# Linear attention and two MLPs on one core: rank of the weight sums and place of the key products

## The chip, the cores and the metric

The kernel runs on one core of a Trainium2 chip. The metric is the time of one execution on the device in microseconds (us), here as the median of several runs. The profile is one further execution, recorded instruction by instruction.

## What is computed

```python
kv  = einsum('bhsd,bhse->bhde', k, v)           # 8 batches, 8 heads, 576 rows, 64 columns
out = einsum('bhsd,bhde->bhse', q, kv)
x   = out / sqrt(mean(out**2, -1) + 1e-6) * g_norm
x   = x.transpose(0, 2, 1, 3).reshape(4608, 512)
h   = x @ w_in                                  # first MLP, 512 -> 2048 -> 512
g   = where(h >= 1, h, where(h <= -1, 0, (h + 1)**2 / 4))
x   = g @ w_out
h   = x @ w_in2                                 # second MLP, same sizes
out = maximum(h, 0)**2 @ w_out2
```

The weights come in as float64 and are narrowed on the chip; the rest is float32.

## The kernel before

**Blocks and pairs.** The 4608 rows are nine blocks of 512. Blocks 0 to 4 of the first MLP are computed plainly: for each of 16 slices of the hidden width, `h_stage` (line 686) makes 12 matmuls into a PSUM bank, then ScalarE and VectorE form the gate u (lines 704 to 706), `g_stage` (712) splits it into a high and a low part (gs), and `out_stage` (729) makes 12 more matmuls into four accumulators, two slices behind. Two rounds of hooks stand in one slice: a half slice is called a slot, so a block has 32 slots. The rest (blocks 5 to 8 of the first MLP, all of the second) is computed in pairs of blocks, with seven block products instead of eight (`in_phase`, 904, and `out_phase`, 969). For these pairs sums of quarters of the weights are needed.

**The weight sums.** They are made during blocks 1 to 4, in 16 units (`units`, line 1127; the loop that hooks them stands at 1134 to 1154). A unit loads two raw slices of the second MLP's weights (`prep_load`, 313), narrows them (`prep_narrow`, 345, through `narrow_w`, 267: one ScalarE and two VectorE instructions each, lines 272 to 275), forms four sums (`prep_sums`, 357: four VectorE instructions, lines 362 to 366), splits four tiles (`prep_split`, 369, through `split_halves`, 185: one ScalarE and one VectorE instruction each, the latter at line 189), and then does the same for the first MLP's weights, which lie in SBUF already: `prep_join` (332, line 342) adds their two parts again, `prep_sums`, and two splits. For the last slices of `w_out` the parts come back from DRAM, as tiles wf and wt. Each split tile is stored to DRAM (wsd) from ScalarE's queue two slots later (`owe` and `pay`, 173 to 182). The split tiles go round a ring of SBUF slots (`prep_ring`), which the tiles e of the first pair take over (`e_pairs`, line 776).

**The attention.** A block's attention is computed while the block before it runs, and that of blocks 5 to 7 inside the first two pairs ("hosted": two groups of six pairs of heads). `attention` (652) gives every job a slot: pair of heads j has its base s, 7 slots behind the one before it (6 in the hosted groups). At s - 7 the loads of k and v, at s the key product `kv_stage` (474; from block 2 on one call serves two pairs of heads, j and j + 1, and stands at j's slot) and the transpose of q, at s + 3 and s + 4 the two halves of the output (`o_stage`, 570: product po, squares, scaling), at s + 6 the sums of squares `r_stage` (596): product pr for two halves, logarithm (609), exponential (611), square, a Newton step on VectorE (526) that reads pr once more, and the normalisation. So the sums of squares of pair j - 1 stand at s - 1 of pair j (at s in the hosted groups, in front of j's key product). The product pkv is evicted in four pieces, each a ScalarE copy and a VectorE subtraction into kvbd (lines 497 to 499); po reads kvbd.

**Banks.** From block 1 on, pkv, po and pr all take their PSUM bank from one pool of two (`bank`, 397, tag `at`).

**What sets the order.** Each instruction has a rank, which counts up as the program is traced. When the program is built, the instructions of each engine are put in order by a planner that plays the program through: of the instructions that it holds to be ready it takes the one with the lowest rank. The order is fixed from then on; on the chip each engine and each DMA queue goes through its list and waits at its head.

Of the kernel before, what the change touches and what calls it, by code (L numbers as in the profile page):

```python
# [77 lines left out]
def linear_attention_rms_two_mlps(  # L78
# [19 lines left out]
    NF = DFF // P  # L98
# [5 lines left out]
    LAG = 2  # L104
    AHEAD = 3
    WARM = 11
    PACE = 0.75
    WAVE = 6
    WHOLE = ((1, 0), (1, 1))
    WARMS = ((0, 5), (6, 5), (8, 3), (12, 4), (14, 3), (20, 3), (26, 3))  # L110
# [22 lines left out]
    PLAIN = 5  # L133
# [518 lines left out]
    def attention(base, every, order):  # L652

        slots = []
        for j, (b, hp) in enumerate(order):
            s = base + int(every * j)
            turn.setdefault((b, hp), len(turn))
            if b == 1:
                slots += [(max(0, s - 7), load_kv, b, hp), (s, kv_stage, (b, hp))]
            elif j % 2 == 0:  # L660
                two = order[j : j + 2]
                turn.setdefault(two[-1], len(turn))
                slots += [(max(0, s - 7), load_kv, *i) for i in two]
                slots.append((s, kv_stage, *two))
            slots += [
                (max(0, s - (7 if b < PLAIN or j < 2 else 5)), load_q, b, hp),
                (s, t_stage, b, hp),
                (s + 3, o_stage, b, hp, 0),
                (s + 4, o_stage, b, hp, 1),
            ]  # L670
            if j == 0 and b < PLAIN:
                slots.append((s + 6, begin, b))
            slots.append((s + 6, r_stage, b, hp))
        if b < PLAIN:
            slots.append((2 * NF * b, store_xrem, b))
        return slots
# [398 lines left out]
    def outputs(n, hn, hm):  # L1075
# [21 lines left out]
                stores.append((rows[a], src))  # L1097
        return stores

    blocks = [(1, b) for b in range(PLAIN)]  # L1100
    hooks = {}

    def hook(s, f, *a):
        hooks.setdefault((s // 2, s % 2), []).append((f, a))

    jobs = [(8, store_xrem, 0)]
    for b in range(1, PLAIN):
        jobs += attention(2 * NF * (b - 1), 7, [(b, hp) for hp in range(NP)])
# [25 lines left out]
    for which, i, s0, j in [  # L1134
        (which, i, 2 * NF * (n + 1) + s, 4 if s in (0, 6, 12) else 6)
        for n in range(PLAIN - 1)
        for which, i, s in units[n]
    ]:
        for d, L, f, a in (
            (-6, 2, prep_load, ()),  # L1140
            (0, 2, prep_narrow, (0,)),
            (1, 2, prep_narrow, (1,)),
            (2, 2, prep_sums, ()),
            (2, 2, prep_split, (0,)),
            (3, 2, prep_split, (1,)),
            (3, 2, prep_split, (2,)),
            (4, 2, prep_split, (3,)),
            (2, 1, prep_load, ()),
            (j, 1, prep_join, ()),
            (j + 1, 1, prep_sums, ()),  # L1150
            (j + 1, 1, prep_split, (2,)),
            (j + 2, 1, prep_split, (3,)),
        ):
            hook(min(s0 + d, 2 * NF * PLAIN - 1), f, L, which, i, *a)

    first_x = x2_jobs(0, Ring(*[(st, "st")] * 7))
    when = [2, 3, 3, 4, 5, 6, 7, 8, 7, 9, 9, 10, 11, 12, 13, 14]
# [5 lines left out]
    for n in HOSTED:  # L1163
        for s, *job in sorted(attention(1, 6, HOSTED[n]), key=lambda j: j[0]):
            if s:
                in_pair.setdefault((n, s), []).append(job)
            elif n:
                in_pair.setdefault((n - 1, 14 * NQ - 4), []).append(job)
            else:
                hook(last + 25, *job)  # L1170
# [17 lines left out]
    for j in range(2):  # L1188
        s = slice(j * D, (j + 1) * D)
# [140 lines left out]
```

## Time and profile before

| | before |
|---|---|
| median of 3 runs | 1578.89 us (1577.68 to 1579.36) |
| profiled execution | 1579.17 us |
| its span, first to last instruction | 1577.4 us |
| TensorE busy | 98% |
| VectorE busy | 76% |
| ScalarE busy | 59% |
| mean granted clock of TensorE | 0.998 |

PE is TensorE's matmul, PEld its weight load, DVE VectorE, ACT ScalarE, SP the queue that issues most loads; a q behind an engine's name is its sequencer. L242 and the like are lines of the kernel (L242 and L880 are helpers that issue the matmuls of the blocks and of the pairs, L189, L221, L228 and L809 helpers for splits, copies and squares). An arrow to the left leads from what is written to what is read. Behind a wait stands what ended it.

### The profile page before, as it was taken

How to read it: one execution, taken by the hardware profiler on the slowest of the kernel's cores; microseconds unless marked ns; L12 is line 12 of the kernel's file. 1: busy time of each engine (PE TensorE's matmuls, PEld its weight loads, DVE VectorE, ACT ScalarE, POOL GpSimd, SP SyncE). 2: the span in 40 equal slices, each digit the busy share in tenths (PEclk: the TensorE clock that was granted, in tenths of full speed). 3: DMA queues.
4: the chain of work that ended last, by engine and by line, in shares of the span. 5: the costliest groups of instructions: out<-in, count | busy, mean ns of one | idle time of the engine just before them, and what ended most of it. 6: DMA issues, size and time to landing. Idle time of an engine off the chain costs nothing.

```text
span 1577.4 us, 22371 instructions
## 1 busy us (share of the span) xinstructions
PE 1542.1 (98%) x7631; PEld 1265.3 (80%) x7633; DVE 1196.6 (76%) x2112; ACT 929.3 (59%) x1751; POOL 13.0 (1%) x30
## 2 busy tenths in 40 slices
PE   9999899999999999998999999999999999999999
PEld 5787778878877788786778888888888888888899
DVE  6975878887989678965599788868884597559676
ACT  5976666766756567735576466546653464446354
POOL 0000000000000000000000000000000000000000
PEclk9999999999999999999999999999999999999999
DMA  9676899796899967778667877766777676977797
GB/s 284 201 246 200 263 319 317 247 286 207 271 346 348 323 202 223 243 211 239 197 211 233 224 244 236 227 218 195 245 225 212 196 244 196 244 239 226 218 390 247
DMA packets 330914, 388.17 MB, mean 246 GB/s; under 512 B 197808, under 2 KB 223408, under 8 KB 330800
## 3 DMA queue, kind: packets, MB, share of 16 engines
q1 hardware_dynamic: 299904, 330.63, 69.2%
q10 hardware_dynamic: 30896, 56.11, 9.5%
q8 instruction: 61, 1.00, 0.3%
q14 instruction: 53, 0.43, 0.1%
HBM read 300.42 MB, written 86.25 MB: 245 GB/s over the span
## 4 chain that ended last, share of the span: by engine, by line
PE 81%; DVE 8%; ACT 5%; DMA 4%; issue 1%; SPq 0%; ACTq 0%; DVEq 0%
PE ph L880 32%; PE po L880 28%; PE acc L242 9%; PE ph L242 8%; DMA ws<-wsd 1%; PE pkv L486 1%; PE po L242 1%; DMA wsd<-s 1%; DVE s L189 1%; PE pr L608 1%; DVE u L706 1%; DVE t L809 1%; DMA v<-in_v_dram 1%; DVE x L809 1%; DVE t L526 1%
## 5 line engine op out<-in xcount | busy, mean ns | idle before, releaser
L880 PE MATMUL ph<-x,ws 128*128 128x512 f32 (+1 forms) x2352 | 507.3, 376 | 0.5 <-DVE u L706 0.5
L880 PEld LDWEIGHTS ph<-x,ws 128*128 128x128 f32 x2352 | 419.6, 189 | 80.0 <-DVE u L706 0.9
L880 PE MATMUL po<-t,ws 128*128 128x512 f32 x2016 | 463.6, 390 | 1.6 <-DVE t L809 1.2
L880 PEld LDWEIGHTS po<-t,ws 128*128 128x128 f32 x2016 | 376.4, 188 | 84.7 <-DVE t L809 6.7
L809 DVE TENSOR_TENSOR t<-g,t 128x512 fp32r<-128x512 f32 (+1 forms) x336 | 216.0, 649 | 82.7 <-ACT t L221 75.9
L221 ACT CAST t<-g 128x512 fp32r<-128x512 f32 (+1 forms) x336 | 195.2, 590 | 115.9 <-PE po L880 62.2
L242 PE MATMUL ph<-x,w 128*128 128x512 f32 x960 | 240.2, 394 | 6.0 <-DVE u L706 4.5
L242 PEld LDWEIGHTS ph<-x,w 128*128 128x128 f32 x960 | 177.0, 188 | 49.3 <-DVE u L706 9.3
L242 PE MATMUL acc<-gs,w 128*128 128x512 f32 x528 | 133.3, 394 | 2.5 <-DVE u L706 1.5
L957 ACT ACTIVATE g<-h 128x512 f32<-128x512 f32 (+1 forms) x120 | 70.6, 589 | 99.0 <-DVE h L946 98.8
L242 PEld LDWEIGHTS acc<-gs,w 128*128 128x128 f32 x528 | 97.4, 188 | 24.5 <-DVE u L706 2.0
L946 DVE CUSTOM_DVE_ANT_0 h<-ph,e 128x512 f32<-128x512 f32 (+1 forms) x120 | 76.1, 637 | 53.5 <-PE ph L880 49.5
L936 DVE TENSOR_TENSOR e<-ph,e 128x512 f32<-128x512 f32 (+1 forms) x112 | 72.3, 650 | 57.1 <-PE ph L880 48.4
L242 PE MATMUL acc<-gs,wt 128*128 128x512 f32 x432 | 105.2, 390 | 2.8 <-DVE gs L234 1.7
L242 PEld LDWEIGHTS acc<-gs,wt 128*128 128x128 f32 x432 | 80.4, 188 | 19.9 <-DVE gs L234 2.1
L221 ACT CAST x<-xr 128x512 fp32r<-128x512 f32 (+1 forms) x98 | 57.4, 590 | 46.7 <-DVE xr L860 23.1
L221 ACT CAST gs<-u 128x512 fp32r<-128x512 f32 x80 | 49.8, 622 | 51.4 <-DVE u L706 42.3
L706 DVE SCALAR_TENSOR_TENSOR u<-u,ph 128x512 f32<-128x512 f32 x80 | 54.6, 682 | 22.7 <-ACT u L228 22.5
L704 ACT ACTIVATE u<-ph,halfb 128x512 f32<-128x512 f32 x80 | 55.3, 691 | 27.0 <-PE ph L242 17.4
L234 DVE TENSOR_TENSOR gs<-u,gs 128x512 fp32r<-128x512 f32 x80 | 55.0, 688 | 16.4 <-ACT gs L221 15.9
L933 ACT COPY e<-ph 128x512 f32<-128x512 f32 (+1 forms) x56 | 30.6, 553 | 58.6 <-PE ph L880 51.7
L809 DVE TENSOR_TENSOR x<-xr,x 128x512 fp32r<-128x512 f32 (+1 forms) x98 | 63.1, 648 | 2.5 <-ACT x L221 2.5
(135 smaller groups left out, 1620.7 us busy)
## 6 DMA issues: line engine op xcount, KB each, us to landing
ws<-wsd SPq DMA_DIRECT2D x392, 512.0 KB, 4.4
wsd<-s ACTq DMA_DIRECT2D x96, 512.0 KB, 5.6
wt<-wsd SPq DMA_DIRECT2D x36, 512.0 KB, 5.4
raw<-in_moe_w_in_dram SPq DMA_DIRECT2D x32, 512.0 KB, 6.9
raw<-in_moe_w_out_dram SPq DMA_DIRECT2D x32, 512.0 KB, 6.3
xr<-x1d SPq DMA_DIRECT2D x36, 256.0 KB, 5.3
out_dram<-ov SPq DMA_DIRECT2D x142, 64.0 KB, 3.7
wsd<-w SPq DMA_DIRECT2D x17, 512.0 KB, 4.0
```

What stands on the lines that cost most here:

```text
L189: lo.tensor_tensor(t[:, :, 1, :], src, t[:, :, 0, :].bitcast(F32), ALU.subtract)
L221: return e.copy(dst, src)
L234: lo = engine(op + "_lo", phase).tensor_tensor(t[:, 1, :], src, t[:, 0, :].bitcast(F32), ALU.subtract)
L242: nc.tensor.matmul(dst, wt(a), xt(c), start=first and n == 0, stop=last and n == 2)
L704: nc.scalar.activation(u, ps, AF.Relu, bias=halfb, scale=0.5)
L706: nc.vector.scalar_tensor_tensor(u, u, 1.0, ps, op0=ALU.min, op1=ALU.max)
L809: engine2(op + "_lo").tensor_tensor(t[:, 1, :], src, t[:, 0, :].bitcast(F32), ALU.subtract)
L880: nc.tensor.matmul(ps, wt(a), xt(c), start=first and n == 0 and i == 0, stop=last and n == len(lhs) - 1 and i == 2, skip_group_check=True,)
L933: nc.scalar.copy(e[i, 1], bank)
L936: nc.vector.tensor_tensor(e[i, p], bank, e[i, 1], ALU.add)
L946: nc.vector._custom_dve(TENSOR_ADD_SAT, out=h, in0=bank, in1=add, s0=float("inf"), s1=0.0)
L957: nc.scalar.activation(g, h, AF.Square)
```

## The change

Three edits. The 16 units' instructions, apart from the loads, are traced by way of `behind`, which gives them a rank 60 higher than the place at which they are traced. A key product that serves two pairs of heads, unless it is its group's first, is put one slot earlier in the hosted groups and two slots earlier in blocks 2 to 4, so that it is traced ahead of the sums of squares of the pair of heads before it. A constant that nothing reads (`PACE`) is replaced by `BEHIND`.

```diff
-    PACE = 0.75
+    BEHIND = 60
...
-                slots.append((s, kv_stage, *two))
+                slots.append((s - (1 if j else 0) - (b < PLAIN and j > 0), kv_stage, *two))
...
+    def behind(f, *a):
+        with tc.high_priority(offset=-BEHIND):
+            f(*a)
+
...
-            hook(min(s0 + d, 2 * NF * PLAIN - 1), f, L, which, i, *a)
+            if f is not prep_load:
+                f, a = behind, (f, L, which, i, *a)
+                hook(min(s0 + d, 2 * NF * PLAIN - 1), f, *a)
+            else:
+                hook(min(s0 + d, 2 * NF * PLAIN - 1), f, L, which, i, *a)
```

## Rows read from the trace of the kernel before

**Rows 1.** The page, busy time, share of the span and instructions

```profile
PE 1542.1 (98%) x7631; PEld 1265.3 (80%) x7633; DVE 1196.6 (76%) x2112; ACT 929.3 (59%) x1751; POOL 13.0 (1%) x30
```

**Rows 2.** Stretches (us): length, busy time of each engine, clock, DMA share, GB/s

```profile
core 0: us, PE busy (x) PEld busy (x) DVE busy (x) ACT busy (x) POOL busy (x), PEclk, DMA share, GB/s
...
125.70:235.00 109.30, 100.87 (x534) 79.53 (x532) 76.53 (x145) 68.91 (x136) 4.17 (x4) 1.00 0.86 269
235.00:335.00 100.00, 99.59 (x527) 82.11 (x527) 82.69 (x158) 69.72 (x139) 1.93 (x5) 1.00 0.90 281
...
431.30:523.30 92.00, 90.74 (x425) 72.72 (x424) 80.16 (x153) 58.77 (x106) 0.00 (x0) 1.00 1.01 347
...
710.00:830.00 120.00, 108.39 (x543) 88.53 (x542) 83.92 (x138) 70.76 (x144) 0.00 (x0) 0.97 0.76 218
```

**Rows 3.** TensorE's waits in block 1, 125.7 to 235: total, times, longest

```profile
PE ph L242 <- DVE u L706: 2.9, 4, 1.4
PE pr L608 <- ACT wk L213: 1.7, 2, 1.0
...
PE pr L608 <- DVE s2lo L594: 1.1, 1, 1.1
...
PE pkv L486 <- DVE t L526: 0.4, 1, 0.4
```

**Rows 4.** TensorE's waits in block 4 and behind it, 431.3 to 531

```profile
PE acc L242 <- DVE gs L234: 1.7, 1, 1.7
PE ph L242 <- DVE u L706: 1.2, 3, 0.7
```

**Rows 5.** TensorE's waits in the hosted stretch, 700 to 830

```profile
PE pkv L486 <- DVE t L526: 5.7, 2, 3.1
...
PE po L242 <- DVE kvbd L499: 1.4, 1, 1.4
PE po L242 <- ACT kvbd L221: 1.4, 1, 1.4
```

**Rows 6.** A stretch of the pairs, 900 to 1000, as rows 2

```profile
900.00:1000.00 100.00, 99.87 (x439) 81.78 (x438) 87.15 (x140) 64.27 (x107) 0.00 (x0) 1.00 0.78 240
```

**Rows 7.** TensorE in order of time, 738 to 757: start, length, in brackets idle before

```profile
744.75 0.56 PE L486 MATMUL pkv<-kv 128*64 128x64 f32 x10 [3.11 <-DVE t L526]
...
752.34 1.01 PE L242 MATMUL po<-qT,kvbd 128*128 128x288 f32 x3 [1.40 <-ACT kvbd L221]
```

**Rows 8.** The same, 786 to 797

```profile
785.82 2.90 PE L880 MATMUL ph<-x,ws 128*128 128x512 f32 x12
...
791.59 0.69 PE L486 MATMUL pkv<-kv 128*64 128x64 f32 x16 [2.61 <-DVE t L526]
...
792.69 0.29 PE L486 MATMUL pkv<-rest 128*64 128x64 f32 x4
```

**Rows 9.** Two stretches behind TensorE's waits, as rows 2

```profile
745.60:749.00 3.40, 3.40 (x10) 2.63 (x9) 2.25 (x4) 0.37 (x1) 0.00 (x0) 0.50 1.01 407
...
755.80:759.30 3.50, 3.50 (x10) 2.73 (x9) 0.76 (x1) 0.99 (x3) 0.00 (x0) 0.51 0.00 0
```

**Rows 10.** VectorE in order of time, 792 to 799.5

```profile
798.74 0.23 DVE L499 TENSOR_TENSOR kvbd<-pkv,kvbd 64x64 fp32r<-64x64 f32 x1
```

**Rows 11.** TensorE in order of time, 183 to 186

```profile
183.81 0.69 PE L486 MATMUL pkv<-v,k 128*64 128x64 f32 x16
```

**Rows 12.** SP's queue in order of time, 171 to 178.5

```profile
175.69 0.60 SPq L433 DMA_DIRECT2D rest<-in_v_dram  x1
```

**Rows 13.** The tile rest, 160 to 190

```profile
DMA to landing us min/median/max: 2.7/3.0/3.2
```

**Rows 14.** Groups of VectorE's instructions, 125.7 to 530: busy, mean ns | idle before

```profile
L189 DVE TENSOR_TENSOR s<-s,s 128x512 fp32r<-128x512 f32 x62 | 42.0, 684 | 13.7 <-ACT s L221 13.6
```

**Rows 15.** VectorE in order of time, 518 to 540

```profile
525.46 0.69 DVE L342 TENSOR_TENSOR j<-wt 128x512 f32<-128x512 f32 x1 [4.29 <-DMA wt<-wsd]
...
537.71 0.69 DVE L936 TENSOR_TENSOR e<-ph,e 128x512 f32<-128x512 f32 x1 [3.84 <-DMA wsd<-s]
```

## The prediction

> **What bounds the kernel now.** I read the shares of the engines first. TensorE is busy 1542.1 of 1577.4 us [rows 1], so all that a change of order can win is about 35 us, of which the first load and the last eviction keep some 5. The stage table says where TensorE loses time: 8.4 us in block 1 (109.30 long, 100.87 busy), 0.4 in block 2, 1.3 in block 4, 11.6 in the stretch 710 to 830 that carries the second half of the hosted attention; VectorE is at 70 to 87% in these stages, so it has slack on average and is late only in places [rows 2]. The waits of TensorE name the places. Block 1 waits for u and for the operands of the sums of squares [rows 3]; the end of block 4 waits once for gs and three times for u [rows 4]; the hosted stretch waits 5.7 us in two places for the key product's bank, and 2.8 for the split of its result [rows 5]. These waits, not an engine's total, set the end: TensorE's stream is fixed work with holes.
>
> A rule bears on how much room there is. In 900 to 1000 us, where TensorE is busy 99.87 of 100, its weight loads are busy 81.78 [rows 6]; 80% over the whole span [rows 1] is thus already the full pace. The Trainium skill (Perfetto Trace Analysis, Identifying the Most-Contended Engine) says that matmul busy time is no good measure of the distance to the roofline and that the share of LDWEIGHTS is; by it a fifth of the span, some 312 us, would be open, by the row only the 35.
>
> **The key product.** One product serves two pairs of heads. In each of the two hosted groups of six pairs, the second and the third product are moved one slot forward (4 in all); of blocks 2 to 4 each has its second product moved two slots (3, which run in blocks 1 to 3). Each brings 40 small matmuls, 4 ScalarE and 4 VectorE pieces of its eviction; its loads stay where they are. Nothing is added.
>
> Today the product is traced behind the sums of squares of the pair before. It needs one of the two attention banks, and these are held until VectorE's Newton step has read the sums of squares (L526), at the end of a chain of logarithm, exponential and square. So TensorE stands 3.11 us at 741.6 and 2.61 us at 789.0 [rows 7, 8]. In front of the sums it takes the bank of the output's first half, which ScalarE freed earlier: both waits go, -5.7 us.
>
> The first of them costs more than itself. Behind it the clock of TensorE is granted at 0.50 for 3.4 us, though it is busy throughout, and again at 0.51 for 3.5 us behind the two waits of 1.4 us [rows 9]; behind the 2.61 us wait it isn't. At 0.50 (1.2 instead of 2.4 GHz) 3.4 us hold 1.7 us of work, so each such stretch costs 1.7. The first goes with its wait: -1.7. The second, and the 2.8 us of waits on the split before it, come from a product that was late and evicted late; one slot (12 matmuls, 2.7 us, rows 8) earlier it should be out, unless ScalarE takes the pieces as late as now. Between 0 and -4.5 I take half: -2.3.
>
> What is late next is the second half of the sums of squares. Its bank can only be the key product's, since the first half's is held until both halves are through the chain. Today four pieces are out 7.4 us after the product starts (791.59 to 798.97) [rows 8, 10], in the middle of other work. The builder may put 12 or more other matmuls between, so the price is from 0 to 3.3 us each (7.4 less the product's own 1.4 and a slot of 2.7). I take 0.5, because TensorE's order is chosen at build time with these waits in view: 4 x 0.5 = +2.0.
>
> In blocks 2 to 4 the gain is the one wait there, 0.4 [rows 3]. Against it stand the loads: the product of block 2 runs at 183.81, but the last of its loads is issued at 175.69, and these land 3.2 us later at the slowest, 178.9 [rows 11 to 13]. Two slots, some 6 us, earlier it asks for them at 177.8: a wait of 1.1, with bounds of 0 and 4.6 (in front of the sums of squares, traced in the slot between, it could start as early as 174.3). In the other two blocks the loads land long before. Net +0.7.
>
> **The sums.** 16 units, each 8 ScalarE and 20 VectorE instructions, get a rank 60 traced instructions later, about two slots; one split piece takes 0.68 us [rows 14]. Their loads keep their rank, and so do the stores that ScalarE's queue issues, which now can wait there for a later split. A rank decides only where the builder finds several instructions ready; there u, gs and the attention now go first. Engine time doesn't change, VectorE's slack takes the delay, so I cost the delay itself at nothing in blocks 1 to 3; without that cover each late store would hold up a ring slot and the next unit. The gain is taken from the waits on u and on the sums of squares in block 1 and on u in block 4, 2.9 + 1.7 + 1.1 + 1.2 = 6.9 us [rows 3, 4]. A wait goes only where a sum stood in front at that moment; half: -3.4, between 0 and -6.9.
>
> At the end of block 4 I give nothing for the 1.7 us wait for gs. VectorE sits 4.29 us on a tail weight that the join of the last unit reads, with gs queued behind; yet 12 us later it sits 3.84 us until that unit's store has freed the slot that e of the first pair writes [rows 15]. TensorE gains 1.7 at the first place and arrives earlier at the second, which still hangs on the same load. If the last splits slip behind two more operations, 2 x 0.68, TensorE pays that: +1.4, between 0 and about 3.
>
> **The sum**: -5.7 - 1.7 - 2.3 + 2.0 + 0.7 - 3.4 + 1.4 = -9.0. The profiled execution took 1579.2 us (span 1577.4), 0.3 above the median of 1578.9, so the forecast is **1570.0 us**, -0.6%. About 0.2% (3.2 us) is what a measurement of this kernel can tell from no change.
>
> **Rivals.**
> (a) The ranks do nothing: sums stand where they stand because their inputs arrive when they do (the 4.29 us wait is one for a load, rows 15), not because of a tie. Then the last two terms fall away: -5.7 - 1.7 - 2.3 + 2.0 + 0.7 = -7.0, 1572. For it: blocks 2 to 4 have few waits with the same sums in them. Against: the wait on u in block 1, beside an idle that no load explains. Still faster.
> (b) The wait changes place: the second half of the sums waits 2 us at each of the four hosted products (8 us instead of the 2.0 that I charged) and the 2.3 doesn't come: 1570.0 + 6.0 + 2.3 = 1578.3. For it: two banks, and an eviction of 7.4 us. Against: TensorE's order is free to put other matmuls in.
> (c) Slower, by the same bank where the eviction stays as slow as the row: each of the four second halves waits the full 3.3 us, 13.2, and two of these waits lower the clock, 3.4. Against the forecast that is 13.2 - 2.0 + 3.4 = +14.6: 1584.6. It decides from where a wait passes about 2.7 us without the clock: 4 x 2.7 is the hosted gain of 9.7 and 1.3 from the sums. That is a product whose last piece comes over 6.8 us behind its start. For it: the 7.4 measured. Against: that eviction stood behind a late product, with nobody pressing it. The Trainium skill (Perfetto Trace Analysis, Matmuls) wants independent groups to rotate through banks so that the eviction of one overlaps the matmuls of the next; with two banks the moved product breaks that rotation, which speaks for this rival. No row of before shows a sum of squares behind a key product.
>
> **Chances.** The forecast's case 0.54 (1563 to 1575), (a) 0.14 (1570 to 1575), (b) 0.16 (1575.7 to 1582), (c) 0.16 (above 1582). Faster by over 0.2% is the first two, 0.68; within 0.2% 0.16; slower 0.16. Its best end is all of the hosted waits and clock (11.9) and most of the others: 1561. The range of 1561 to 1581 holds the first two cases and nearly all of (b), and leaves out (c); the forecast's own range is 1563 to 1575.
>
> **What would show it.** Right: no wait of a key product for L526 in the hosted stretch, the clock there at 1.00 instead of 0.97, and TensorE's idle time between 710 and 830 down from 11.6 to some 3; in block 1 waits on u under 1.5. Wrong, step by step: a wait of pr for kvbd (the bank's price is larger than 0.5); a wait of the key product for a load near 178 us (two slots too early); VectorE's order in block 1 with the sums still in front (the rank does nothing); a longer idle than 3.84 in front of the first pair's e with TensorE waiting behind (the late sums set the first pair's start). If idle of TensorE turns up in stages that now have none, the new order itself, which none of these terms holds, has made it.

## The result, and the profile after

The changed kernel is slower: median 1588.03 us (1586.32 to 1590.83) against 1578.29 us for the kernel before (1576.46 to 1579.36); ratio 1.0066, 95% interval 1.0051 to 1.008. By the ratio that is +10.4 us where -9.0 was forecast, and outside the range. The profiled execution took 1586.32 us, its span 1584.5, against 1577.4; mean granted clock 0.992 against 0.998.

The page's first part says that no engine got more to do; it answers to [rows 1].

```profile
PE 1542.3 (97%) x7633; PEld 1270.4 (80%) x7633; DVE 1198.8 (76%) x2112; ACT 932.3 (59%) x1751; POOL 10.4 (1%) x30
```

TensorE has the same busy time and 7 us more idle time. Where, the stretches from stage to stage show: block 1, block 4, the first pair with the first hosted group, and the 120 us behind it. Their columns are those of [rows 2].

```profile
core 0: us, PE busy (x) PEld busy (x) DVE busy (x) ACT busy (x) POOL busy (x), PEclk, DMA share, GB/s
125.92:233.15 107.23, 99.34 (x504) 79.84 (x502) 75.34 (x142) 68.45 (x133) 1.69 (x4) 0.98 0.84 269
...
430.35:526.54 96.19, 91.79 (x425) 74.37 (x424) 82.21 (x155) 58.40 (x103) 0.00 (x0) 0.98 0.96 333
526.54:711.01 184.47, 175.98 (x849) 144.35 (x848) 144.22 (x243) 107.77 (x212) 0.00 (x0) 0.97 0.76 233
711.00:831.00 120.00, 109.93 (x582) 89.72 (x581) 78.88 (x133) 68.41 (x141) 0.00 (x0) 0.97 0.74 209
```

The same stages in the kernel before, cut at the same matmuls of the blocks and pairs:

```profile
125.69:234.93 109.24, 100.81 (x534) 79.47 (x532) 76.47 (x145) 68.85 (x136) 4.17 (x4) 1.00 0.86 268
...
431.25:523.36 92.11, 90.85 (x425) 72.79 (x424) 80.20 (x153) 58.82 (x106) 0.00 (x0) 1.00 1.01 348
523.36:700.49 177.13, 174.13 (x849) 142.62 (x848) 141.77 (x237) 105.67 (x207) 0.00 (x0) 1.00 0.78 238
```

Block 1 gains 2.0 us, block 4 loses 4.1, the first pair loses 7.3, blocks 2 and 3 lose 0.4 each, and from the start of the second hosted group to the end 3.4 are gained (1577.4 - 700.49 against 1584.5 - 711.01). With 0.2 at the start that is the 7.1 of the span. Blocks 1 and 2 belong together: 30 small matmuls of a key product stand ahead of the cut between them in the kernel before and behind it in the changed kernel (534 and 504 instructions in block 1). And of the 3.4 only 1.5 are gained in the hosted group: counted by the matmuls of the pairs, the changed kernel is 10.5 us behind at 700, 9.1 at 849 and 7.1 at 1191 us of the kernel before, and between the last two no attention is computed. So the loss stands where the forecast had a +1.4, and the hosted gain, forecast at 7.7, is 1.5 in these two traces.

**The first pair.** TensorE's waits between 420 and 560 have one of 7.8 us that the kernel before does not have:

```profile
PE ph L880 <- DVE e L936: 7.8, 1, 7.8
PE ph L242 <- DVE u L706: 4.1, 3, 2.1
```

VectorE between 536 and 553, in order of time (idle before in brackets), stands in front of e for a store, as in [rows 15], but twice as long:

```profile
536.59 1.89 DVE L189 TENSOR_TENSOR s<-s,s 128x512 fp32r<-128x512 f32 x3 [0.71 <-ACT s L221]
546.39 0.69 DVE L936 TENSOR_TENSOR e<-ph,e 128x512 f32<-128x512 f32 x1 [7.91 <-DMA wsd<-s]
```

ScalarE's queue over the same time issues the stores of these splits:

```profile
535.92 1.67 ACT L221 CAST s<-s 128x512 fp32r<-128x512 f32 x3
537.31 2.69 ACTq L181 DMA_DIRECT2D wsd<-s  x3
```

The last unit's two splits end at 538.5, their stores are the last two of the three (issued at 539.0 and 539.5), and only when the first of these has landed is the ring slot free that e wants: e stands 7.4 us behind its issue. In the kernel before that store is issued at 532.04 and e stands at 537.71 [rows 15], 5.7 us behind it. The wait costs more than itself. Stretches as in [rows 9], the first behind a 2.05 us wait for u in block 4, the second behind this one, are at half the clock:

```profile
467.00:470.40 3.40, 3.40 (x10) 2.65 (x9) 3.40 (x7) 2.06 (x5) 0.00 (x0) 0.51 1.04 407
...
542.00:552.20 10.20, 5.07 (x12) 4.01 (x13) 3.53 (x8) 3.84 (x9) 0.00 (x0) 0.50 0.64 222
```

5.07 busy us at half the clock hold 2.5 us of work. 7.8 + 2.5 less the 1.7 that the kernel before waits for gs [rows 4] is 8.6, somewhat over the 7.3 that the stage lost (5.5 more idle and 1.9 more busy, by the rows above).

**The hosted stretch.** The two waits of the key product [rows 7, 8] are gone, and two others have come, seen in TensorE's order of time:

```profile
751.00 0.69 PE L486 MATMUL pkv<-kv 128*64 128x64 f32 x16
...
752.31 0.40 PE L608 MATMUL pr<-s,ones 128*128 128x288 f32 x1
752.55 0.29 PE L608 MATMUL pr<-s2lo,ones 128*128 128x288 f32 x1
752.68 2.91 PE L880 MATMUL ph<-x,ws 128*128 128x512 f32 x12
755.42 0.35 PE L608 MATMUL pr<-s,ones 128*128 128x288 f32 x1
...
759.79 0.67 PE L242 MATMUL po<-qT,kvbd 128*128 128x288 f32 x2 [3.89 <-ACT qT L221]
...
800.00 0.40 PE L608 MATMUL pr<-s,ones 128*128 128x288 f32 x1 [3.45 <-DVE kvbd L499]
```

At 800.00 the second half of the sums of squares waits for the key product's bank, as feared. At 752.68 it does not wait: the builder put 12 matmuls in between. But then the second half reads its squares (tile s2, tag wk2) 3 us later, and the transposed q of the next pair of heads goes into that same buffer:

```profile
755.35 1.29 DVE L946 CUSTOM_DVE_ANT_0 h<-ph,e 128x512 f32<-128x512 f32 x2
756.55 0.77 DVE L565 STREAM_TRANSPOSE qf<-q 128x576 f32<-128x576 f32 x1
```

In the kernel before that transpose runs at 741.76, 3.0 us ahead of the key product at 744.75; here 5.6 us behind it, and the output's product waits 3.89 us for it. At the second place VectorE is seen waiting, in front of the transpose, for the matmuls that read s2:

```profile
800.44 0.78 DVE L565 STREAM_TRANSPOSE qf<-q 128x576 f32<-128x576 f32 x1 [0.49 <-PE pr L608]
```

The 3.89 us are not the buffer's alone: the transpose ends at 757.3, and ScalarE casts its result only at 759.03, behind an exponential, a gate step and a square. In block 1 a wait of 4.25 us for the transposed q stands at 193.12.

**ScalarE in blocks 1 to 4.** A gate is two instructions on ScalarE, lines 704 and 228 (u), and ScalarE also issues the stores. Its waits in front of the second, 125 to 530, before:

```profile
ACT u L228 <- DMA v<-in_v_dram: 3.3, 1, 3.3
...
ACT u L228 <- ACT u L704: 0.7, 2, 0.4
```

and after:

```profile
ACT u L228 <- DVE s L189: 7.2, 7, 2.3
...
ACT u L228 <- DVE j L342: 5.2, 2, 3.1
ACT u L228 <- DMA wsd<-s: 4.7, 1, 4.7
...
ACT u L228 <- DVE s L366: 2.5, 1, 2.5
...
ACT u L228 <- DVE d L274: 1.6, 1, 1.6
```

4.0 us have become 23.4 (the rows left out are of 1.1, 0.9 and 0.2). The square needs none of the five shown: what stands between it and line 704 in ScalarE's list is a store, which waits, mostly for its split (in the row of 4.7, and in the 3.3 of before, for an earlier transfer to land). The stores kept their rank while the splits got a later one. In the list as built, 8 of the 64 gates of blocks 1 to 4 have such a store inside before, 27 after.

### The profile page after: what moved, and what is told of

Same layout as the page of the kernel before. It is cut to its first block, busy times and chain, and to the rows that moved or that the text cites. A ratio compares the mean times of both kernels' runs of the same rounds, so it can differ in the third digit from the quotient of the medians.

```text
span 1584.5 us, 22442 instructions
## 1 busy us (share of the span) xinstructions
PE 1542.3 (97%) x7633; PEld 1270.4 (80%) x7633; DVE 1198.8 (76%) x2112; ACT 932.3 (59%) x1751; POOL 10.4 (1%) x30
## 4 chain that ended last, share of the span: by engine, by line
PE 83%; DVE 6%; DMA 5%; ACT 4%; issue 1%; ACTq 0%; SPq 0%; DVEq 0%
PE ph L880 31%; PE po L880 28%; PE acc L242 10%; PE ph L242 9%; DMA wsd<-s 2%; DMA ws<-wsd 2%; PE po L242 1%; PE pkv L486 1%; PE pr L608 1%; DVE t L809 1%; PE pwarm L1191 1%; DVE x L809 1%; DMA rest<-in_k_dram 1%; DVE s L189 0%; ACT raw L272 0%
```

## The experiments

Each expectation was written before its run. The ratios are to runs of the kernel before on the same chip. Taken alone, the parts give:

| what differs from the kernel before | median us | ratio, 95% interval | ratio less 1, in us |
|---|---|---|---|
| the change | 1588.03 | 1.0066, 1.0051 to 1.008 | +10.4 |
| key products alone (e1) | 1579.49 | 1.0005, 0.9996 to 1.0015 | +0.8 |
| ranks alone (e2) | 1586.93 | 1.0048, 1.0034 to 1.0062 | +7.6 |
| ranks of blocks 1 to 3 alone (e14) | 1583.26 | 1.0021, 1.001 to 1.0032 | +3.3 |
| ranks of block 4 alone (e13) | 1584.03 | 1.0029, 1.002 to 1.0039 | +4.6 |
| rank of the last unit alone (e8) | 1578.77 | 1.0001, 0.9992 to 1.001 | +0.2 |

The second, fourth and fifth row make 8.7 together, inside the interval of the change (8.0 to 12.6).

### Key products alone, ranks alone

e1 is the kernel before with the changed line in `attention` alone; e2 with `behind` alone.

> Only the key products are moved; the sums keep the rank of before. Theory (late sums cost the time, the key products bring some 3 us in the hosted stretch): 1576 us, between 1573 and 1579, no wait of over 4 us of TensorE on e at the start of the first pair, and the waits of po for qT (4.2 in block 1, 3.9 in the hosted stretch) still there. Rival (the key products cost the time, since they push the sums of squares and with them the next transpose back): 1586 us or more, as the changed kernel.

Measured 1579.49 us, ratio 1.0005: nothing gained, between theory and rival. The hosted waits are those of the changed kernel (3.89 and 3.46), and nothing waits long for e. The moved products take two waits away and put two as long in their place. The wait for q's transpose in block 1, which the theory expected as well, is not there: it comes in runs that have both parts (the change, e3 with 4.25, e4 and e5), and in neither part alone.

> Only the sums get the later rank; the key products stand where they stood. Theory: the last unit's store comes some 7 us later than before, TensorE waits about 8 us on e at the start of the first pair and loses 5 more to the clock behind it: 1591 us, between 1586 and 1595. Rival (the key products cost it): 1576 to 1580 us.

Measured 1586.93 us, ratio 1.0048. TensorE waits 7.58 us for e at 540.29 and 4.34 for u at 463.57, and in the hosted stretch as before (3.11, 2.60, 1.40, 1.43). The loss is the ranks'. A first theory, on record together with these two, was that it is nearly all the ring's, some 13 us of wait and clock.

### The ring and the last unit, with the rest of the change

```diff
-    hook(last + 1, prep_ring.add, *((xp, f"x{KD + i}") for i in range(KD)))
+    def turn_ring():
+        prep_ring.slots[:] = [(wp, "w1_15")] + [(xp, f"x{KD + i}") for i in range(KD)]
+        prep_ring.slots += [(wp, f"w1_{i}") for i in (12, 13, 14)]
+
+    hook(last + 1, turn_ring)
```

e3 is the changed kernel with this: the tiles e of the first pair's products 6 and 7 go to slots whose splits were stored earlier. e4 is the changed kernel with block 4's units at their old rank (`if f is not prep_load and s0 < last`).

> The changed kernel, except that the ring of SBUF slots for the split sums is turned, so that the first pair's e tiles take the slots of sums that were stored earlier; the sums are as late as in the changed kernel. Theory (the slot is what TensorE waits for): the 7.8 us wait on e and the 10 us at half clock behind it go, 12.9 us less: 1575 us, between 1573 and 1579. Rival (the late sums hold the first pair up in another way, by engine time of VectorE or by the weights' loads): 1584 us or more.

> The changed kernel, but the units of block 4 keep their old rank; those of blocks 1 to 3 are late as in the changed kernel. Theory: both the wait on e (12.9 us with the clock) and most of the 4 us that block 4 lost go: 1572 us, between 1569 and 1577. Rival (the delay of earlier units pushes the last ones back as well): 1582 us or more.

e3: 1581.28 us, ratio 1.0016 (1.0006 to 1.0026). The wait for e falls from 7.77 to 0.78, and by the ratios (1.0066 and 1.0016) 7.9 us of the 13 that I expected come back. e4: 1582.83 us, ratio 1.0028 (1.0017 to 1.0039): no long wait for e (0.39), but 2.88 and 2.01 for gs and 2.05 for u in block 4 and right behind it. Both stay above the kernel before. The first theory was half of it: the ring's share is 7.9 us here, 3.8 without the moved key products (e2 against e10, below), and something is left that neither touches.

e7 is the kernel before with the turned ring, a control.

> The kernel before with the turned ring alone. Theory: VectorE's 3.8 us idle in front of the first pair's e goes, but TensorE did not wait there: 1577 us, between 1575 and 1580. Rival (the ring itself brings several us, so the gain of the run with the turned ring is not that of the late sums alone): 1573 us or less.

1578.94 us, ratio 0.9998 (0.9988 to 1.0008). Without the later ranks the ring is worth nothing; TensorE still waits for gs (2.97 us at 525.4) and comes late to e.

### The stores

e5 is e3 with the stores of the splits at the later rank too.

```diff
-                nc.scalar.dma_start(dst, src)
+                with tc.high_priority(offset=-late):
+                    nc.scalar.dma_start(dst, src)
```

> As the run with the turned ring, and the stores of the split sums are traced with the later rank as well, so that they stand behind the gates in ScalarE's list again. Theory (in blocks 1 to 4 ScalarE's queue stands at a store whose split is late, with the square of a gate behind it): ScalarE's waits in front of the square of u fall from 23 us to under 10, TensorE's waits for u fall from 9 to under 5, and the time from 1581 to 1577 us, between 1574 and 1579. Rival (VectorE's own order makes the gates late): no change, 1580 to 1583 us.

1585.88 us, ratio 1.0043 (1.0027 to 1.0059): no better than e3, if anything worse, and outside the theory's range. What it was to do it did: none of ScalarE's waits in front of u's square is for a split or a store any more, and TensorE's waits for u between 125 and 530 fall from 11.3 us in e3 to 4.5. But beside them stand a wait of 3.70 for a load of v at 493.8, one of 2.71 for u at 529.2 and one of 1.41 for q's transpose at 313.8, none of which e3 has. That the stores hold up ScalarE is shown; that letting them through gains time is not.

### Which sums

```diff
-            hook(min(s0 + d, 2 * NF * PLAIN - 1), f, L, which, i, *a)
+            if f is not prep_load and s0 == last + 25:
+                f, a = behind, (f, L, which, i, *a)
+                hook(min(s0 + d, 2 * NF * PLAIN - 1), f, *a)
+            else:
+                hook(min(s0 + d, 2 * NF * PLAIN - 1), f, L, which, i, *a)
```

This is e8, the last unit alone. e13 has `s0 >= last` there (the five units of block 4), e14 `s0 < last` (the eleven of blocks 1 to 3), e10 all 16 with the turned ring.

> The kernel before with the later rank for the six steps of the last unit of block 4 alone; every other sum and all key products stay. Theory (the store of the last unit's late third split frees a ring slot late, and the first pair pays for it, 7.8 us of wait and then half the clock): TensorE waits 7 to 8 us for e at about 540 us, half clock behind it, 1585 us (1583 to 1588), nearly the whole loss of the changed kernel. Rival (the loss is the sum of many gates in blocks 1 to 4): 1580 us or less, with a wait for e of under 3 us.

> All sums of blocks 1 to 4 with the later rank, key products where they were, and the turned ring. Theory: the wait for e goes, what is left is ScalarE waiting in front of u's square for late splits: 1580 us (1578 to 1583), still not under the kernel before. Rival 1 (with the ring out of the way the ranks bring what was forecast for them, 3.4 us): 1575. Rival 2 (the ring helps only with the key products moved): 1585 or more.

> The later rank for the five units of block 4 alone, key products and ring as before. The last unit alone cost nothing, so the third split of that unit must be late because the other sums of block 4 slip in front of it. Theory: the wait for e is 5 us or more, a wait of 3 us or more for u beside it in block 4, 1584 us (1582 to 1587). Rival (the store is late only because the earlier blocks' units slipped too, and push block 4's): wait for e under 3.5 us, 1581 or less.

> The later rank for the eleven units of blocks 1 to 3 alone, key products and ring as before. Theory (ScalarE's stores wait for late splits in front of u's square, so that u is late at several gates): no gain in block 1, waits for u there of 1 to 3 us as in the run of the ranks alone, 1582 us (1580 to 1584). Rival (the early blocks win what was forecast, 1.5 to 2.5 us, and the loss of the ranks is all block 4's): 1577 (1575.5 to 1578).

e8, 1578.77 us, contradicts the theory that the last unit's own rank makes its third split late. The wait for gs is gone and a shorter one for e has come:

```profile
PE ph L880 <- DVE e L936: 2.2, 1, 2.2
```

e13, 1584.03 us, has the long wait. TensorE's waits of 125 to 560, and VectorE in order of time:

```profile
PE ph L880 <- DVE e L936: 7.6, 1, 7.6
PE ph L242 <- DVE u L706: 5.0, 6, 1.5
```

```profile
529.39 0.42 DVE L362 TENSOR_TENSOR s<-wf,j 128x256 f32<-128x256 f32 x1
...
531.54 1.90 DVE L189 TENSOR_TENSOR s<-s,s 128x512 fp32r<-128x512 f32 x3 [0.82 <-ACT s L221]
541.11 0.69 DVE L936 TENSOR_TENSOR e<-ph,e 128x512 f32<-128x512 f32 x1 [7.68 <-DMA wsd<-s]
```

So the other four units of block 4 push the last unit's store back, and the first pair pays. (The four without the last were not run.) The push is smaller than the wait: the store that e waits for is issued at 533.73, 1.7 us later than in the kernel before, it holds the slot 1.7 us longer, and e stands 3.4 us later (541.11 against 537.71, [rows 15]). The other 4.2 of the 7.6 us are TensorE's, which gets to this place earlier, with the wait for gs gone. In e10 the turned ring takes 0.0048 down to 0.0024 (1582.81 us, 1.0015 to 1.0034), as its theory had it; e14 loses 0.0021 without touching block 4. TensorE's waits in block 1 of e14, 125 to 235:

```profile
PE ph L242 <- DVE u L706: 4.5, 4, 1.8
PE acc L242 <- DMA wt<-wsd: 2.9, 1, 2.9
```

In the kernel before the first is 2.9 [rows 3]; the forecast wanted it halved. The waits for the sums of squares are gone, as forecast (1.7 and 1.1 in [rows 3]), but the wait for u and one for a tail weight (1.1 us in the kernel before) grew in their place: all of TensorE's waits there sum to 7.8 us, 8.6 in the kernel before. 0.0029 + 0.0021 is 0.0050, and e2 has 0.0048: the two halves of the ranks add up.

### The key products in the blocks alone

```diff
-                slots.append((s, kv_stage, *two))
+                slots.append((s - 2 * (b < PLAIN and j > 0), kv_stage, *two))
```

> The second key products of blocks 2 to 4 alone, two slots earlier; the hosted ones and all sums stay. Theory (the product holds the second bank, so the sums' second half and with it q's transpose and its buffer come later): the wait of the output's product for q's transpose in block 1 (2 us or more) and the clock behind it, 1580 us (1579 to 1582). Rival (in the blocks the move is harmless, as was forecast, +0.7 - 0.4): 1579 (1578 to 1580), with no wait over 1.5 us in block 1 that the kernel before does not have.

1581.03 us, ratio 1.0006 (0.9995 to 1.0018): between the two, undecided. The wait for q's transpose in block 1 does not come here; one of 2.83 us for u does, at 226.99, as in e1 (2.49). With e1 at 1.0005, nothing is left for the hosted half of the move, which was not run alone: no gain that can be measured, and no loss. The 1.5 us that the trace gained in the hosted group, and the 1.9 behind it, are one execution's; the ratios don't bear them out. Whether the earlier product would pay if the transposed q had a buffer of its own was not tried.

### The key products later instead of earlier

e6 is the kernel before with the hosted products one slot later by rank.

> The kernel before, with the hosted key products that the change moves one slot forward moved one slot back instead: behind the sums of squares with a slot of matmuls between. Theory (the product needs a bank that the Newton step frees 3.1 us behind the sums, and a slot of 2.7 us covers that, while in front of the sums it only hands the wait on): the two waits of 3.1 and 2.6 us and the slow clock behind the first go, the waits on kvbd stay or grow by up to 2 us each: 1573 us, between 1570 and 1578. Rival (two banks are too few in any order, the wait moves to po): 1577 to 1582 us.

1580.32 us, ratio 1.001 (1.0002 to 1.0019). It tested nothing: with the later rank the builder still put the product directly behind the sums of squares, with waits of 3.11 and 2.60 as before; why it did isn't shown. e11 holds it back by force, behind the matmul of the pair that was traced last.

```diff
+    latest = []
+
+    def kv_later(*pairs):
+        with tc.issue_after(latest[-1].ins):
+            kv_stage(*pairs)
...
-                slots.append((s, kv_stage, *two))
+                hosted = b >= PLAIN and j > 0
+                slots.append((s + hosted, kv_later if hosted else kv_stage, *two))
...
-                nc.tensor.matmul(
+                latest[:] = [nc.tensor.matmul(
```

> The kernel before; the second and third key product of each hosted group stands one slot later instead of earlier, held behind the latest matmul of the hosting product, so that some 12 other matmuls lie between the sums of squares and the product that wants their bank. Theory (the waits of 3.1 and 2.6 us come from the bank being asked for too soon behind the sums, and the waits that replace them are those of the output's products for the split of the key product's result, up to 2 us each): 1575 us (1573 to 1577.5). Rival (with two banks and two buffers the wait only moves to the output's product or to q's transpose, whatever the order): 1578 to 1582.

1571.08 us, ratio 0.9947 (0.9935 to 0.9959), better than its theory. TensorE in order of time:

```profile
741.60 0.30 PE L614 MATMUL pr<-s2lo,ones 128*128 128x288 f32 x1
741.73 2.92 PE L887 MATMUL ph<-x,ws 128*128 128x512 f32 x12
746.09 3.01 PE L887 MATMUL ph<-x,ws 128*128 128x512 f32 x12 [1.43 <-DMA ws<-wsd]
749.03 0.69 PE L486 MATMUL pkv<-kv 128*64 128x64 f32 x16
...
750.35 5.74 PE L887 MATMUL ph<-x,ws 128*128 128x512 f32 x24
755.92 0.55 PE L242 MATMUL po<-qT,kvbd 128*128 128x288 f32 x3
```

The chain behind the sums of squares ends under the 24 matmuls that now follow them, the product finds its bank, and its eviction ends under the 24 that follow it. What is left of the waits on kvbd between 710 and 830 is 0.7 us (2.8 in [rows 5]). The stretch, as in [rows 2]:

```profile
710.00:830.00 120.00, 112.82 (x576) 91.73 (x575) 90.38 (x151) 75.49 (x154) 0.00 (x0) 1.00 0.81 235
```

TensorE is busy 4.4 us more of the same 120, and the clock stays at 1.00 instead of 0.97 (two stretches of 3.4 us at half less, [rows 9], which is 3.4 us of work). That is 7.8 of the 8.4 us by the ratio. New are two waits for weights, 1.9 us together, one of them in the rows above; and elsewhere, near 176 and 528, the clock of this execution fell twice, where that of the kernel before did not.

### What beats both

e9 is e8 with the turned ring, e12 that with e11.

> The same, with the ring of the first pair turned so that its sixth and seventh products write slots that were freed long before. Theory: the wait for e is gone, and so is the wait for gs at the end of block 4, since the join that stands on a late load no longer stands in front of gs: 1576 us (1574 to 1579), faster than the kernel before by 2 to 3. Rival (the gate loses at the end of block 4 for another reason, or the time comes back as a wait in the first pair): 1579 to 1582.

> The later key products of the hosted groups and, of the ranks, the last unit's alone with the turned ring. Theory (two separate places, 220 us apart, so the gains add up): 1579 - 8.1 - 2.8 = 1568 us (1566 to 1570.5). Rival (the gate of the gs wait and the ring were worth something only by where the clock fell, so that one takes the other's gain): 1570.5 to 1573.

e9: 1576.41 us, ratio 0.9981 (0.9972 to 0.999). The waits for gs and for e at the end of block 4 are both gone but for this, 431 to 560:

```profile
PE ph L242 <- DVE u L706: 1.3, 4, 0.4
PE ph L880 <- DVE e L936: 0.8, 1, 0.8
```

Here the place where a sum that waits for a load stood in front of a gate, the 4.29 us of [rows 15], is corrected alone. e12: 1566.84 us, ratio 0.9919 (0.9902 to 0.9936), 12.8 us faster than the kernel before by the ratio. 0.0019 and 0.0053 would give 0.0072: the gains add up. The hosted stretch is that of e11:

```profile
710.00:830.00 120.00, 113.37 (x570) 91.85 (x568) 92.36 (x155) 77.52 (x159) 0.00 (x0) 0.99 0.82 241
```

## Why the prediction was wrong

**The key product, -5.7 and -1.7: right in the trace, given back.** Both waits on the Newton step went. The forecast said what would be late next, the second half of the sums, and charged 0.5 us each. It waited long once, 3.45 us, just over the upper bound of 3.3. The eviction at 751.00 takes 4.3 us to the last piece (755.32) instead of the 7.4 taken from [rows 8, 10], as was argued against rival (c); the second product, cut in two by 12 other matmuls, is out at 799.95, 5.1 us behind its second part and 8.4 behind its first. What failed is "the builder may put 12 or more other matmuls between", booked as the cheap end. It is not cheap: it moves the second half back by 3 us, and with it the buffer of the transposed q. I had followed the banks and not the buffer s2. That is rival (b) with another tile: the wait changes place. 5.7 us of waits on the Newton step and 2.8 on the split went; 3.89 and 3.45 came. e1 shows the sum, 0.8 us instead of -7.0. The -2.3 came in part: the waits on kvbd did go, but the clock fell twice in the hosted stretch here too, behind the 3.89 and the 3.45.

The Trainium skill (Perfetto Trace Analysis, Matmuls) wants independent groups to rotate through banks so that one's eviction lies under the next one's matmuls. The runs agree, in a way that the forecast did not use: the rotation is restored by putting the product further from the sums (e11, -8.4 us), not by bringing it nearer.

**The loads of block 2's product, +0.7.** The wait of 1.1 us did not come: the product starts at 179.90, some 4 us earlier and not 6, behind the 178.9 by which the loads were to land. e15 (+1.0 us, with an interval from -0.8 to +2.8) leaves open whether the move in the blocks costs anything.

**The sums, -3.4: wrong in sign.** "I cost the delay itself at nothing in blocks 1 to 3" is the first step that failed: VectorE has slack, but the price is not VectorE's. I wrote that ScalarE's stores now can wait for a later split and drew no term from it. e14 measures it: +3.3 us with blocks 1 to 3 alone, with the store inside 15 gates instead of 8. That these stores make all of the 3.3 isn't shown: e5, which moves them, was no faster, and TensorE's waits in e14 are no longer in block 1 and 2.7 us longer behind it (235 to 560: 7.5 and 4.8). Most of the 3.3 goes with the clock: its mean is 0.993 in the middle of e14's 12 runs and 0.995 in that of the 29 runs of the kernel before beside them; (1 - clock) x span is 11.1 and 7.9 us (an estimate of what half clock costs, too high where TensorE was idle). The prediction had no clock term for the ranks; what brings the clock down in e14 stays open.

**The end of block 4, +1.4 with bounds of 0 to 3: right mechanism, wrong size.** The slot, the store and the tile e were named, the wait was the one to look for, and it came. I let two operations slip, 2 x 0.68 us. In fact the other units of block 4 slip too: e13 measures +4.6 us, with e 3.4 us later, and removing the ring's share from the change (e3) gives back 7.9. Two things were left out: the whole queue of sums in front of the last unit moves, not the last splits alone; and the clock is at half in and behind the wait in all three traces that have it (10.2 us in the changed kernel and e13, 6.8 in e2).

**The rivals.** Slower had a chance of 0.16, by (c), a bank in the hosted stretch. The loss did not come from there. The sentence that would have found it stands among the signs of error ("a longer idle than 3.84 in front of the first pair's e"), without a price or a chance.

## What to carry over

A rank that comes later for a whole class of work delays the last piece of it by all the pieces before it; look at what waits for that last piece (here a ring slot behind a store) and delay only the unit that stands in somebody's way (e9). A store in a compute engine's queue that keeps its rank while its split gets a later one holds up the engine; the later rank for the store too took these waits away, but no time (e5). When a wait on a bank is to go, put other work between producer and consumer by force (e11) before swapping the two, and follow every buffer of the stage that slips, not only the bank.

## What the runs showed of the hardware that was not expected

Whether the clock falls behind a wait is not settled by the wait, nor by the program. It falls behind the 2.05 us in block 4 of the changed kernel. Behind the 2.61 us of [rows 8] it does not fall in the kernel before, but it does in e7, where the same wait stands in front of the same product, at 792.69. Just behind it, before and e7:

```profile
792.00:795.40 3.40, 3.40 (x45) 2.91 (x42) 3.32 (x6) 2.19 (x5) 0.00 (x0) 1.00 0.27 92
793.70:797.10 3.40, 3.40 (x21) 2.71 (x17) 3.26 (x8) 1.99 (x6) 0.00 (x0) 0.50 0.28 92
```

e6, e8 and e9 go with e7 here, e2, e10, e13 and e14 with the kernel before. In e12 it falls behind waits of 0.8 and 1.0 us near 174; in the kernel before the same two waits stand there and it stays at 1.00, although up to block 4 the two kernels have the same instructions in the same order. The stretch 177 to 180, e12:

```profile
177.00:180.00 3.00, 3.00 (x9) 2.46 (x9) 3.00 (x7) 3.00 (x8) 0.00 (x0) 0.50 0.85 179
```

and the kernel before:

```profile
177.00:180.00 3.00, 2.68 (x13) 1.91 (x11) 3.00 (x6) 3.00 (x7) 0.00 (x0) 1.00 0.91 188
```

So a clock term that is read from one trace, as the -1.7 was, is one execution's. The mean clock differs from run to run of one kernel: the 105 runs of the kernel before beside the experiments have 0.991 to 0.998, and its profiled execution, with 0.998, is at their upper end. A difference between two kernels' clocks is to be read from many runs: e11's five have 0.997 or 0.998, the 27 of the kernel before beside them 0.995 in the middle; by (1 - clock) x span that is 3.1 against 7.9 us, over half of its 8.4 (an estimate).

And a store of a split tile holds its slot for long: from its issue to the next writer of the slot it is 7.4 us in the changed kernel and in e13, 5.7 in the kernel before.
